# Sliding-window attention and a gated FFN: the values with their operands exchanged, and batch 0 taken unit by unit

## The chip, the core and the metric

The kernel runs on one core of one Trainium2 chip. A core has TensorE (matrix products, results into PSUM), VectorE, ScalarE and GpSimd (elementwise work), and queues that start transfers between the main memory (HBM) and the on-chip memory (SBUF, 128 partitions). The engines run side by side and wait for each other by semaphores. The metric is the device time of one execution in microseconds (us). In the profile the engines are called PE, DVE, ACT and POOL in this order; PEld is the loading of TensorE's stationary operand.

## What is computed

```python
# q, k, v: (8 batches, 8 heads, 576 positions, 64 wide), fp32
scores = (1/8) * q @ k.T                       # per batch and head
mask   = (rel >= 0) & (rel < 64)               # rel = query position - key position
attn   = softmax(where(mask, scores, -1e9))
a      = attn @ v
x      = a.transpose(0, 2, 1, 3).reshape(4608, 512)       # tokens x (heads * 64)
out    = (maximum(x @ w_gate, 0) * (x @ w_val)) @ w_out   # 512 -> 1536 -> 512, fp32
```

Each query sees only the 64 keys up to its own position. A block of 64 queries therefore needs 128 keys: the 64 before the block and the block's own.

## The kernel before

All 4608 tokens are cut into 24 units of 192 positions (three to a batch, all 8 heads) and 12 FFN tiles of two units (384 tokens). The operands are fp16, sums are fp32. The program gives each engine its order of instructions through a small scheduler: `W.at(t, fn)` puts the attention's steps at planned times between the matmuls of the FFN, which move the plan's clock forward; `ready(n)` makes the FFN wait until n units are finished.

For a unit, the scores come out with the keys on the partitions (so p has 128 keys x 64 queries for each window and head), in four row tiles of TensorE, since k and q lie in 32 partitions a head with the 64 channels in pairs:

```python
nc.tensor.matmul(d["st"][hh][g][:, c:c + 64],                        # L249
                 kT[rows, hh, ks + 64*w:ks + 64*w + 128, dh],        # rows: 32 partitions of head g
                 qT[rows, hh, ks + 64*w:ks + 64*w + 64, dh], ...)    # every second fp16 element
```

ScalarE takes the exponential into `p` (`u_exp`), VectorE multiplies by the band mask (`u_mask`). The values are then made with v stationary and p moving. v stands beside 64 columns of ones, so that one product gives the values of a head in 64 output partitions and the sum of p, repeated, in the other 64:

```python
def u_pv_wide(u):                       # 24 matmuls, units 2 to 23
    ...
    nc.tensor.matmul(d["pv"][c % 2][:, c // 2, e, 64*w:64*w + 64],   # L311
                     v16[:, w, 128*h - 64*e:128*h - 64*e + 128],     # 128 x 128 stationary: v and ones
                     d["p"][h % G][:, h // G, 64*w:64*w + 64], ...)  # 64 columns moving

def u_copy(u, n):    # ScalarE: values from PSUM to SBUF, twice two of 64 x 384             (L329)
def u_sum(u, half):  # VectorE: transposes the sums 32 x 32 out of PSUM, 64 x 384 each      (L341)
def u_back(u):       # VectorE: reciprocal of 24 numbers a partition, transposed back       (L348, L350)
def u_norm(u):       # VectorE: xt = values * reciprocal, 128 x 768, to fp16                (L356)
```

The result `xt` has the channels on the partitions, as the FFN needs them (`xt` is `[128, 4, 384]`: 4 groups of 128 channels). The units 0 and 1 do the same with other tiles of PSUM and separate matmuls with ones. v is loaded by windows of 64 keys into the upper 64 partitions, and `v_low` copies it to the lower 64 for the next window.

The FFN of a tile:

```python
def hidden(t, c0, c1, f0=0, f1=NF, each=1):    # NF = 12 blocks of 128 hidden columns
    ...
    nc.tensor.matmul(h[...], wt[:, c, 128*(f + b):128*(f + b) + 128],     # L419, wt: wg or wv
                     xt[:, c, c0:c1], start=(c == 0), stop=(c == NC - 1))
    # ScalarE: r_sb = relu(h of wg)    (L404);   VectorE: g_sb = r_sb * h of wv    (L407)

def output(t, subs):                           # 3 x 12 matmuls of 512 columns, g_sb stationary (L433)
    # ScalarE copies the result, the SP queue stores it
```

The start: k of batch 0 comes in fp32 whole, q of batch 0 whole with conversion to fp16 in the transfer; both are transposed by VectorE for all 576 positions; units 0 and 1 follow, then the FFN of the first half of tile 0.

```python
for hh in range(2): k_first(hh)
for hh in range(2): qk_load(0, "q", hh)
...
W.advance(13.7)
ready(1)
hidden(0, 0, U, 0, 4, 4)
ready(2)
hidden(0, U, TT, 0, 4, 4)
hidden(0, 0, TT, 4, NF, 4)
output_by_rows(0)
ready(3)
hidden(1, 0, U)
output(1, (0,))
ready(4)
hidden(1, U, TT)
output(1, (1, 2))
for t in range(2, NU // 2): ...
```

Of the kernel before, what the change touches and what calls it, by code (L numbers as in the profile page):

```python
# [9 lines left out]
FP32 = mybir.dt.float32  # L10
FP16 = mybir.dt.float16
ACT = mybir.ActivationFunctionType
MUL = mybir.AluOpType.mult

# [28 lines left out]
def kernel(  # L43
# [28 lines left out]
    a_16 = ctx.enter_context(tc.tile_pool(name="a_16", bufs=2))  # L72
    a_p = ctx.enter_context(tc.tile_pool(name="a_p", bufs=6))
# [13 lines left out]
    v16s = [persist.tile([128, UB, H, 128], FP16, name=f"v16_{i}") for i in range(UB)]  # L87
    ones0 = consts.tile([128, 64], FP16)
    ones = consts.tile([128, 64], FP16)
    mask = consts.tile([128, 64], FP16)  # L90
    bias = consts.tile([128, 64], FP16)
    ident = consts.tile([128, 128], FP16)

# [21 lines left out]
    def v_ones(i, eng):  # L115
        eng.memset(v16s[i][64 if i == 0 else 0:, 0, :, 64:128], 1.0)
        for w in range(1, UB):
            eng.memset(v16s[i][:, w, :, 64:128], 1.0)  # L118

    def k_zeros():  # L120
        nc.vector.memset(kTs[1][:, :, 0:64], 0.0)

    def constants():
        nc.vector.memset(kTs[0][:, :, 0:64], 0.0)
        nc.vector.memset(v16s[0][0:64, 0], 0.0)
        nc.vector.memset(ones, 1.0)
        nc.vector.memset(ones0, 1.0)
        nc.vector.memset(ones0[0:64], 0.0)
# [6 lines left out]
    def xt_tile(t):  # L135
        if t not in xts:
            xts[t] = x_sb.tile([128, NC, TT], FP16, name="xt")
        return xts[t]
# [4 lines left out]
    def w_load(wt, src, f0, f1, landed):  # L143

        sr = src.rearrange("(c p) n -> p c n", p=128)
        if wt is wo:
            dst, part = wo[:, f0:f1], sr[:, f0:f1]
        else:
            ns = slice(128 * f0, 128 * f1)
            dst, part = wt[:, :, ns], sr[:, :, ns]  # L150
        nc.gpsimd.dma_start(dst, part)
        w_done.update(((wt.name, f), landed) for f in range(f0, f1))
# [17 lines left out]
    def k_first(hh):  # L170

        k32 = nat["k32", hh] = x_sb.tile([128, S // 32 * D], FP32, name="k32", bufs=2)
        nc.sync.dma_start(k32, k[0, G * hh:G * hh + G].rearrange("h (i j) d -> (h i) (j d)", i=32))

    def k_round(hh, part, parts):
        n = S // 32 * D // parts
        if part == 0:
            nat[0, "k", hh] = a_in.tile([128, S // 32 * D], FP16, name=f"k{hh}", bufs=2)
        nc.scalar.copy(nat[0, "k", hh][:, n * part:n * part + n], nat["k32", hh][:, n * part:n * part + n])  # L179
# [8 lines left out]
    def v_load(u):  # L188
        b, uu = divmod(u, UB)
        for w in range(UB):  # L190
            k0 = U * uu + 64 * w
            nc.gpsimd.dma_start(v16s[uu][64:128, w, :, 0:64], v[b, :, k0:k0 + 64].rearrange("h p d -> p h d"))  # L192

    def v_low(u):

        uu = u % UB
        if uu > 0:
            nc.vector.tensor_copy(v16s[uu][0:64, 0, :, 0:64], v16s[uu - 1][64:128, UB - 1, :, 0:64])
        nc.vector.tensor_copy(v16s[uu][0:64, 1:UB, :, 0:64], v16s[uu][64:128, 0:UB - 1, :, 0:64])

    def u_bias(u, gs=range(G)):

        d = units.setdefault(u, {})
        if "st" not in d:
            st_tiles(u)
        d["biased"] = True
        for to in d["st"][0] + d["st"][1] if u == 0 else [d["st"][0][g] for g in gs]:
            n = 1 if u == 0 else 2
            nc.tensor.matmul(to[:, 0:n * U].rearrange("p (n c) -> p n c", c=64), ident,
                             bias[:, None, :].to_broadcast([128, n * UB, 64]),  # L210
                             start=True, stop=False, skip_group_check=True)
# [5 lines left out]

    def st_tiles(u):
        d = units.setdefault(u, {})
        one = lambda name: f_ps.tile([128, 512], FP32, name=name, tag="h")  # L220
        two = lambda name: a_ps.tile([128, 2, 512], FP32, name=name, tag="a")
        if u == 0:
            d["st"] = [[one("st") for _ in range(G)]]
            halves = [two("st") for _ in range(2)]
            d["st"].append([halves[g // 2][:, g % 2] for g in range(G)])
        elif u == 1:
            half = two("st")
            d["st"] = [[half[:, 0], half[:, 1], one("st"), one("st")]] * 2
        else:
            halves = [two("st") for _ in range(2)]  # L230
            d["st"] = [[halves[g // 2][:, g % 2] for g in range(G)]] * 2
        if u == 0:
            d["spare"] = d["st"][1][3][:, 256:512]
            d["st"] = [[x[:, 0:512 if hh == 1 and g == 3 else 256] for g, x in enumerate(row)] for hh, row in enumerate(d["st"])]

    def u_st(u, hhs=(0, 1)):
        d = units.setdefault(u, {})
        kT, qT = kTs[(u // UB) % 2], qTs[(u // UB) % 2]
        biased = "biased" in d
        if not biased:  # L240
            st_tiles(u)
        ks = U * (u % UB)
        for hh in hhs:
            for w in range(UB):
                c = U * (hh if u else 0) + 64 * w
                for dh in range(2):
                    for g in range(G):
                        rows = slice(32 * g, 32 * g + 32)
                        nc.tensor.matmul(  # L249
                            d["st"][hh][g][:, c:c + 64],  # L250
                            kT[rows, hh, ks + 64 * w:ks + 64 * w + 128, dh],
                            qT[rows, hh, ks + 64 * w:ks + 64 * w + 64, dh],
                            start=(dh == 0 and not biased), stop=(dh == 1),
                            skip_group_check=biased)
        d.setdefault("p", [None] * G)
        return 0.49

    def u_exp(u, g, hh=None):
        d = units[u]
        if not hh:  # L260
            d["p"][g] = a_p.tile([128, 2, U], FP16, name="p")
        if hh is None:
            nc.scalar.activation(d["p"][g].rearrange("p h c -> p (h c)"), d["st"][0][g][:, 0:2 * U], ACT.Exp, scale=scale)  # L263
        else:
            nc.scalar.activation(d["p"][g][:, hh], d["st"][hh][g][:, 0:U], ACT.Exp, scale=scale)

    def u_mask(u, g):
        p = units[u]["p"][g]
        p = p.rearrange("p h (w c) -> p (h w) c", w=UB)
        nc.vector.tensor_tensor(p, p, mask[:, None, :].to_broadcast([128, 2 * UB, 64]), MUL)  # L270

    def u_pv(u, cs=(0, 2, 1, 3)):
        if u > 1:
            return u_pv_wide(u)
        d = units[u]
        v16 = v16s[u % UB]
        if u == 0 and cs[0] == 0:
            d["pv"] = [f_ps.tile([128, 2, U], FP32, name="pv", tag="h") for c in cs]
        elif u == 0:
            both = a_ps.tile([128, 2, 512], FP32, name="pv", tag="a")  # L280
            d["pv"] += [both[:, n, 0:2 * U].rearrange("p (s c) -> p s c", s=2) for n in range(2)]
        else:
            halves = [a_ps.tile([128, 2, 512], FP32, name="pv", tag="a") for _ in range(2)]
            d["pv"] = [halves[c % 2][:, c // 2, 0:2 * U].rearrange("p (s c) -> p s c", s=2) for c in range(NC)]
        for c in cs:
            for w in range(UB):
                for e in range(2):
                    h = 2 * c + e
                    nc.tensor.matmul(
                        d["pv"][c][64 * e:64 * e + 64, 0, 64 * w:64 * w + 64],  # L290
                        v16[:, w, h, 0:64], d["p"][h % G][:, h // G, 64 * w:64 * w + 64],
                        start=(w == 0), stop=True, skip_group_check=True)
            for w0, w1, one in ((0, 1, ones0), (1, UB, ones)) if u % UB == 0 else ((0, UB, ones),):
                for e in range(2):
                    h = 2 * c + e
                    nc.tensor.matmul(
                        d["pv"][c][64 * e:64 * e + 64, 1, 64 * w0:64 * w1],
                        one, d["p"][h % G][:, h // G, 64 * w0:64 * w1],
                        start=False, stop=True, skip_group_check=True)
        return 1.2  # L300

    def u_pv_wide(u):

        d = units[u]
        v16 = v16s[u % UB].rearrange("p w h d -> p w (h d)")
        d["pv"] = [a_ps.tile([128, 2, 2, 256], FP32, name="pv", tag="a") for _ in range(2)]
        for c in (0, 2, 1, 3):
            for e in range(2):
# [317 lines left out]
```

The softmax here doesn't subtract the row's maximum and nothing guards it: scores larger than these inputs give would overflow.

## Time and profile before

| | |
|---|---|
| time, median of 3 runs | 339.22 us (339.13 to 339.65) |
| profiled run: time, span from first to last instruction | 339.75 us, 337.9 us |
| granted TensorE clock, mean | 0.994 |
| first matmul of the FFN | 17.00 us |
| last matmul | ends at 334.28 us |
| FFN hidden matmuls, 128 x 384, from the groups | 1024 of them, 326 ns each in the record |
| gate on VectorE, 128 x 384 out of PSUM | 550 ns, 144 of them |
| exponential on ScalarE, 128 x 384 out of PSUM | 492 ns, 92 of them |

How to read it: matmuls are pipelined, so the duration in the record (326 ns) is longer than the distance from one to the next; for the pace take the length of an uninterrupted piece in the chain of work that ended last, divided by its count. A group's line names line, engine, operation, output and input with partitions x elements, then the count, the busy time, the mean of one, and the idle time of the engine just before it with what ended that.

### The profile page before, as it was taken

Reading aid. Unit: us, or ns where it says so; the run is one execution under the profiler, and the core shown is the slowest. Engines: PE = TensorE matmul, PEld = TensorE weight load, DVE = VectorE, ACT = ScalarE, POOL = GpSimd, SP = SyncE. Lnnn points to the kernel's source line nnn. Section 1 sums busy time; section 2 is a strip of 40 time slices with the busy share of each in tenths; the row PEclk is TensorE's granted clock in tenths of the full one; section 3 lists DMA queues with packets and bytes.
Section 4 is the critical chain, followed back from the end, with each engine's and each line's share of the span. In section 5 each row is a group of like instructions: output and inputs, shape, how many; then the busy total and the mean of one; then the engine's idle time right before and its main releaser. Section 6 shows DMA issues by size and latency. Waiting matters only on the chain.

```text
span 337.9 us, 8605 instructions
## 1 busy us (share of the span) xinstructions
PE 325.5 (96%) x3522; PEld 197.3 (58%) x3522; DVE 260.3 (77%) x493; ACT 176.7 (52%) x383; POOL 74.0 (22%) x121
## 2 busy tenths in 40 slices
PE   8699998999999999999999999999999999999995
PEld 4485485856546656655655655654655664664653
DVE  5878878998998874897989974888889874884430
ACT  4546165745636646645555564564564664653321
POOL 8724341250213221320210410150120200000000
PEclk9989999999999999999999999999999999999999
DMA  8999998496343933491242853296214402001002
GB/s 214 178 206 193 204 203 135 31 139 98 24 77 49 158 51 71 29 185 70 17 53 73 111 75 98 18 143 123 17 10 111 32 3 93 2 2 71 24 0 94
DMA packets 52886, 29.44 MB, mean 87 GB/s; under 512 B 39280, under 2 KB 44272, under 8 KB 52848
## 3 DMA queue, kind: packets, MB, share of 16 engines
q0 software_dynamic: 47088, 18.29, 47.4%
q1 hardware_dynamic: 5616, 10.55, 8.7%
q8 instruction: 27, 0.44, 0.6%
q14 instruction: 11, 0.09, 0.1%
q10 hardware_dynamic: 144, 0.07, 0.1%
HBM read 37.75 MB, written 9.44 MB: 140 GB/s over the span
## 4 chain that ended last, share of the span: by engine, by line
PE 81%; DVE 13%; issue 3%; DMA 2%; ACT 0%; DVEq 0%; ACTq 0%; POOLq 0%
PE h L419 52%; PE op L433 21%; PE pv L311 5%; PE st L249 3%; DVE sT L341 2%; DVE qT L186 2%; DMA q<-in_q_dram 2%; DVE g_sb L407 2%; DVE kT L186 1%; DVE xt L356 1%; DVE rs L350 1%; DVE p L270 1%; PE op L465 1%; DVE v L118 1%; DVE rT L348 0%
## 5 line engine op out<-in xcount | busy, mean ns | idle before, releaser
L419 PE MATMUL h<-xt,wg 128*128 128x384 f16 (+1 forms) x640 | 117.5, 313 | 1.7 <-DVE xt L356 1.7
L419 PE MATMUL h<-xt,wv 128*128 128x384 f16 (+1 forms) x640 | 116.7, 311 | 1.0 <-DVE g_sb L407 1.0
L407 DVE TENSOR_TENSOR g_sb<-r_sb,h 128x384 f16<-128x384 f32 x144 | 78.3, 550 | 48.8 <-PE h L419 47.1
L404 ACT ACTIVATE r_sb<-h 128x384 f32<-128x384 f32 x144 | 70.2, 492 | 67.0 <-PE h L419 55.3
L433 PE MATMUL op<-wo,g_sb 128*128 128x512 f16 x420 | 93.0, 379 | 0.0
L192 POOL DMA_DIRECT2D v<-in_v_dram x72 | 49.5, 696 | 181.0 <-PE pv L311 95.3
L419 PEld LDWEIGHTS <-wg 128*128 128x128 f16 x640 | 61.5, 99 | 36.5 <-DVE xt L356 1.6
L419 PEld LDWEIGHTS <-wv 128*128 128x128 f16 x640 | 59.0, 98 | 31.7 <-issue 1.3
L433 PEld LDWEIGHTS <-g_sb 128*128 128x128 f16 x420 | 40.3, 98 | 46.6
L341 DVE STREAM_TRANSPOSE sT<-pv 64x384 f32<-64x384 f32 x88 | 51.1, 580 | 9.7 <-PE pv L311 7.7
L329 ACT COPY xv<-pv 64x384 f32<-64x384 f32 x88 | 41.6, 473 | 21.5 <-DVE sT L341 8.1
L440 ACT COPY o_sb<-op 128x512 f32<-128x512 f32 x35 | 20.5, 586 | 54.6 <-PE op L433 54.6
L263 ACT ACTIVATE p<-st 128x384 f16<-128x384 f32 x92 | 39.7, 492 | 4.2 <-PE st L249 4.1
L270 DVE TENSOR_TENSOR p<-p,mask 128x384 f16<-128x384 f16 x88 | 27.5, 352 | 0.3 <-ACT p L263 0.2
L350 DVE STREAM_TRANSPOSE rs<-rT 128x768 f32<-128x768 f32 x24 | 23.5, 978 | 0.8
L356 DVE TENSOR_TENSOR xt<-xv,rs 128x768 f16<-128x768 f32 x24 | 22.8, 948 | 0.8
L311 PEld LDWEIGHTS <-v 128*128 128x128 f16 x528 | 18.6, 98 | 4.2 <-issue 0.8
L186 DVE STREAM_TRANSPOSE kT<-k 128x576 f32<-128x576 f32 (+1 forms) x18 | 19.7, 1121 | 1.4 <-ACT k L179 1.3
L311 PE MATMUL pv<-p,v 128*128 128x64 f16 x528 | 19.7, 193 | 1.1 <-DVE p L270 0.6
L186 DVE STREAM_TRANSPOSE qT<-q 128x576 f32<-128x576 f32 x16 | 18.9, 1239 | 1.1 <-DMA q<-in_q_dram 1.1
L249 PEld LDWEIGHTS <-kT 32*128 32x128 f16 x1152 | 11.0, 92 | 10.0 <-issue 9.9
L249 PE MATMUL st<-qT,kT 32*128 32x64 f16 x1152 | 13.9, 189 | 2.3 <-DVE qT L186 2.0
(47 smaller groups left out, 91.8 us busy)
## 6 DMA issues: line engine op xcount, KB each, us to landing
out_dram<-o_sb SPq DMA_DIRECT2D x35, 256.0 KB, 2.0
q<-in_q_dram POOLq DMA_DIRECT2D x16, 288.0 KB, 8.1
v<-in_v_dram POOLq DMA_DIRECT2D x72, 64.0 KB, 3.2
k<-in_k_dram POOLq DMA_DIRECT2D x14, 288.0 KB, 6.1
wg<-in_moe_w_gate_dram POOLq DMA_DIRECT2D x3, 512.0 KB, 10.1
wv<-in_moe_w_val_dram POOLq DMA_DIRECT2D x3, 512.0 KB, 11.9
wo<-in_moe_w_out_dram POOLq DMA_DIRECT2D x3, 512.0 KB, 13.7
k<-in_k_dram SPq DMA_DIRECT2D x2, 576.0 KB, 4.0
```

Source lines behind the costliest of these rows:

```text
L186: nc.vector.transpose(dst.rearrange("p (i j) -> p j i", i=32)[:, j0:j1], src[:, j0:j1])
L192: nc.gpsimd.dma_start(v16s[uu][64:128, w, :, 0:64], v[b, :, k0:k0 + 64].rearrange("h p d -> p h d"))
L249: nc.tensor.matmul(d["st"][hh][g][:, c:c + 64], kT[rows, hh, ks + 64 * w:ks + 64 * w + 128, dh], qT[rows, hh, ks + 64 * w:ks + 64 * w + 64 ...
L263: nc.scalar.activation(d["p"][g].rearrange("p h c -> p (h c)"), d["st"][0][g][:, 0:2 * U], ACT.Exp, scale=scale)
L270: nc.vector.tensor_tensor(p, p, mask[:, None, :].to_broadcast([128, 2 * UB, 64]), MUL)
L311: nc.tensor.matmul(d["pv"][c % 2][:, c // 2, e, 64 * w:64 * w + 64], v16[:, w, 128 * h - 64 * e:128 * h - 64 * e + 128], d["p"][h % G][:, ...
L329: nc.scalar.copy(d["xs"][rows, n::2], d["pv"][n][rows, :, e, 0:U])
L341: nc.vector.transpose(to[64 * e:64 * e + 64, half::2], d["pv"][half][64 - 64 * e:128 - 64 * e, :, e, 0:U])
L404: nc.scalar.activation(part(r_sb), part(h1), ACT.Relu)
L407: nc.vector.tensor_tensor(g_sb[:, f:f + w, c0:c1], part(r_sb), part(h2), MUL)
L419: nc.tensor.matmul(h[:, b * n:b * n + n], wt[:, c, (f + b) * 128:(f + b) * 128 + 128], xt[:, c, c0:c1], start=(c == 0), stop=(c == NC - 1))
L433: nc.tensor.matmul(op, g_sb[:, f, bass.ds(sub * 128, 128)], wo[:, f], start=(f == 0), stop=(f == NF - 1))
```

## The change

It exchanges the operands of the value product. p is the stationary operand, 32 queries at a time, and v with one column of ones (65 columns) is moving; four heads stand side by side in the four column tiles of TensorE, so the output has 4 heads x 32 queries on the partitions and the channels, with the sum as the 65th column, along the row. The sum now lies in the partition of its query: the reciprocal and the normalisation need no transposes of sums. The normalised x (fp16) is transposed last, by VectorE, 32 x 32 words of two fp16 channels each. So `xt` becomes `[128, 2, 384, 2]`: a partition holds pairs of neighbouring channels, the FFN reads every second element, and the rows of w_gate and w_val are loaded in the matching order.

v is kept for a whole batch (9 windows of 128 keys, two batches of buffers), loaded by 128 keys for every other window; `v_spread` copies the rest, mostly on GpSimd.

Batch 0 is taken by units: k and q of unit 0 come in fp32 by themselves with all heads, are turned by TensorE (a product with a permuted identity) and copied to `kA` and `qA`; its scores use 64 partitions a head, two row tiles. The units 1 and 2 load and transpose their own parts of k and q. The FFN starts when the units 0 and 1 are both done. Later, the two units of a tile make their values together (`pair`).

```diff
-    a_p = ctx.enter_context(tc.tile_pool(name="a_p", bufs=6))
+    a_p = ctx.enter_context(tc.tile_pool(name="a_p", bufs=12))
-    v16s = [persist.tile([128, UB, H, 128], FP16, name=f"v16_{i}") for i in range(UB)]
+    VW = D + 2
+    v16s = [persist.tile([128, NG, H, VW], FP16, name=f"v16_{i}") for i in range(2)]
-            xts[t] = x_sb.tile([128, NC, TT], FP16, name="xt")
+            xts[t] = x_sb.tile([128, 2, TT, 2], FP16, name="xt")
...  # w_load of wg, wv: two transfers each
+            for a in range(2):
+                nc.gpsimd.dma_start(wt[:, 2 * a:2 * a + 2, ns], src.rearrange("(a p e) n -> a p e n", a=2, e=2)[a, :, :, ns])
...  # u_pv: 48 matmuls a unit
+        for hh in hhs:
+            for w in range(UB):
+                for s in range(2):
+                    for j in range(G):
+                        nc.tensor.matmul(
+                            to[32 * j:32 * j + 32, c:c + D + 1], d["p"][i][:, n, 32 * s:32 * s + 32],
+                            v16s[b % 2][:, vw, G * hh + j, 0:D + 1],
+                            start=True, stop=True, skip_group_check=True)
...  # u_recip, u_norm (twice a unit), u_turn: in place of u_copy, u_sum, u_back, u_norm
+            nc.vector.reciprocal(d["r"], d["both"][...][:, :, :, D:D + 1])
+        nc.vector.tensor_tensor(d["x"][:, hh], pv_of(d, u, hh)[:, :, 0:D],
+                                d["r"][:, hh].to_broadcast([128, SB, D]), MUL)
+        nc.vector.transpose(dst, d["x"][:, h0:h1].rearrange("p a s c -> p a (s c)").bitcast(FP32))
...  # the FFN's moving operand
-                                             xt[:, c, c0:c1], start=(c == 0), stop=(c == NC - 1))
+                                             xt[:, c // 2, c0:c1, c % 2], start=(c == 0), stop=(c == NC - 1))
...  # the start
+        for name in "kq":
+            all_load32(name, 0, nc.sync)
+            all_tile(name, 0)
...
+        for hh in range(2):
+            unit_load(1, "k", hh, 64)
+            unit_load(1, "q", hh)
+        v_load(0, ((1, 0, 128), (3, 0, 64)))
+        v_load(1, ((3, 64, 128), (5, 0, 128)))
+        w_load(*G3[0], 15.2)
+        w_load(*V3[0], 17.8)
+        for hh in range(2):
+            unit_load(2, "k", hh)
+            unit_load(2, "q", hh)
+        w_load(*G3[1], 22.5)
+        v_load(2)
+        w_load(*V3[1], 26.8)
+        w_load(*G3[2], 29.4)
+        w_load(*V3[2], 32.0)
...  # rounding, unit_flip (24 matmuls), unit_keep (copies out of PSUM) for k and q; first_st; unit 1
...  # the plan of the later units
+            W.at(P, lambda: u_pv(2 * t) + u_pv(2 * t + 1))
...
-        W.advance(13.7)
-        ready(1)
-        hidden(0, 0, U, 0, 4, 4)
+        W.advance(15.2)
         ready(2)
-        hidden(0, U, TT, 0, 4, 4)
-        hidden(0, 0, TT, 4, NF, 4)
-        output_by_rows(0)
+        hidden(0, 0, TT, 0, 8, 4)
         ready(3)
-        hidden(1, 0, U)
-        output(1, (0,))
+        hidden(1, 0, U, 0, 4, 4)
+        hidden(1, 0, U, 4, 8, 4)
+        hidden(0, 0, TT, 8, NF, 4)
+        hidden(1, 0, U, 8, NF, 4)
+        output(0)
         ready(4)
         hidden(1, U, TT)
-        output(1, (1, 2))
+        output(1)
```

## The prediction, made before the changed kernel ran

> **What bounds the kernel now.** I read the page's totals first, then the chain that ended last, then the same chain in order of time, then a table of busy times by stage.
>
> ```profile
> PE 325.5 (96%) x3522; PEld 197.3 (58%) x3522; DVE 260.3 (77%) x493; ACT 176.7 (52%) x383; POOL 74.0 (22%) x121
> ...
> PE 81%; DVE 13%; issue 3%; DMA 2%; ACT 0%; DVEq 0%; ACTq 0%; POOLq 0%
> ```
>
> TensorE is busy nearly always and is 81% of the chain; VectorE, with 13%, is the only other engine that holds the end back. So work taken from TensorE shortens the time one for one, and work taken from VectorE only where VectorE stands in the chain. One steady tile of 384 tokens, in the chain in order of time (start, length, what, count):
>
> ```profile
> 101.86 0.65 PE h L419 x4
> 102.51 0.48 PE st L249 x39
> 102.99 4.01 PE h L419 x24
> 107.00 0.70 PE pv L311 x24
> 107.70 7.80 PE h L419 x48
> 115.50 0.48 PE st L249 x39
> 115.98 3.36 PE h L419 x20
> 119.34 0.70 PE pv L311 x24
> 120.04 7.77 PE op L433 x36
> ```
>
> The reader is to see that a tile is a row of TensorE pieces with nothing between. 96 hidden matmuls of 384 columns take 7.80/48 = 0.1625 us each, 15.60 in all; 36 output matmuls take 7.77; a unit's scores 0.48 and its values 0.70. The FFN is 23.37 a tile, 12 x 23.37 = 280.4 us, and the change does not touch that arithmetic. The stages, by the places where the chain changes tile (columns: stretch, length, busy time of each engine, granted clock):
>
> ```profile
> 0.00:17.00 17.00, 12.86 (x214) 7.69 (x215) 11.95 (x28) 8.65 (x22) 13.45 (x27) 0.99 1.31 196
> 17.00:36.46 19.46, 18.96 (x201) 13.91 (x201) 15.30 (x34) 10.40 (x24) 6.47 (x10) 0.92 1.33 201
> ...
> 44.23:74.93 30.70, 28.23 (x445) 22.68 (x444) 26.59 (x53) 17.99 (x39) 11.28 (x19) 1.00 0.89 125
> 74.93:101.86 26.93, 26.42 (x279) 15.14 (x276) 24.35 (x43) 14.34 (x31) 3.41 (x5) 1.00 0.48 70
> 101.86:127.81 25.95, 25.95 (x278) 15.04 (x277) 20.50 (x41) 14.46 (x31) 6.97 (x11) 1.00 0.60 93
> ```
>
> The account of the 337.9 us span: 17.0 before the first FFN matmul (units 0 and 1 are done with TensorE by then), 280.4 of FFN, 22 units x 1.18 = 26.0, 3.6 after the last matmul, and so 10.9 of losses. By stage, length less FFN and units: 17.00 to 36.46 loses 19.46 - 16.78 = 2.7 (8% of it is the clock, 0.92: 1.6); 44.23 to 74.93 loses 30.70 - 26.91 = 3.8 (VectorE busy 26.6 of 30.7: it is the limit there); 74.93 to 101.86 loses 1.2; from there to 310.87, eight tiles, 3.2, of which 0.2 a tile is the change between kinds of matmul (25.95 against 25.73), and the rest the two tiles in which the next q and k are transposed.
>
> **What the Trainium skill says.** "TensorEngine Tiling (Array Packing)", "When to Use Tiling", names just this exchange: with 64 moving columns or fewer, swap stationary and streaming operand and tile by columns. Its "Restrictions" add that column tiling switches the fast weight load off. The trace has one hint: the values of unit 0 use two column tiles of 64, and ten such matmuls (eight of 64 columns, two of 128) come each 0.19 us, 19 ns apiece with a load of 64 columns each; so loads of 64 columns follow at 19 ns or less, and 32 columns should fit in some 10 ns. The same page's "Key Properties" says that a change of tiling mode drains the array; the 0.2 us a tile above fits that, though it is not proof. "SBUF — State Buffer", "Door 1: The DMA port swizzle", says that a strided read runs at full rate while two or more elements are taken from each 16-byte line. The new x is read at every second fp16 element, four per line, so at full rate. In the trace q is already read so by the scores: 48 matmuls of 64 columns in four row tiles take 0.48 us, 40 ns for four abreast, where half rate would need 64 x 2 / 2.4 = 53 ns. Half rate is ruled out, a milder slowdown isn't.
>
> **The change, part by part.**
>
> Values on TensorE. 24 matmuls of 64 columns (29 ns each, 0.70 us) become 48 of 65 columns in four column tiles. Abreast they are 12 groups; 65/2.4 = 27 ns each plus what the 48 issues ask. The scores issue 48 matmuls with 48 loads in 0.48, 10 ns apiece, and I take that: 0.48. Saved 0.22 a unit, 22 units: **4.8 us**, all on the path.
>
> VectorE and ScalarE. What goes:
>
> ```profile
> L341 DVE STREAM_TRANSPOSE sT<-pv 64x384 f32<-64x384 f32 x88 | 51.1, 580 | 9.7 <-PE pv L311 7.7
> L329 ACT COPY xv<-pv 64x384 f32<-64x384 f32 x88 | 41.6, 473 | 21.5 <-DVE sT L341 8.1
> ...
> L350 DVE STREAM_TRANSPOSE rs<-rT 128x768 f32<-128x768 f32 x24 | 23.5, 978 | 0.8
> L356 DVE TENSOR_TENSOR xt<-xv,rs 128x768 f16<-128x768 f32 x24 | 22.8, 948 | 0.8
> ```
>
> Per unit VectorE loses 4 x 0.58 + 0.98 + 0.95 = 4.25 us, and about 0.7 of v copies, which mostly go to GpSimd. It gains two normalisations of 384 elements out of PSUM (the gate of 384 elements takes 0.55: 1.1) and one transpose of 384 fp32 words (from 1.24 for 576 and 0.71 for 288: 0.89); the reciprocal stays near 0.3. Net about 2.9 us a unit, 5.8 a tile: VectorE falls from 20.5 to 24.4 of each 26 us to some 17. ScalarE loses 4 x 0.47 = 1.9 a unit, which was never the limit. Where VectorE was the limit this is worth: 44 to 75, loss 3.8 to 1.0; 75 to 102, 1.2 to 0.4; the eight later tiles, 3.2 to 2.0 (1.6 of changes of mode, 0.4 of batch ends). **4.8 us**.
>
> The start. Before, the first FFN matmul waits for k and q of the whole batch 0 (1.18 MB each in fp32), then transposes, scores, values, sums, and begins at 17.00 with unit 0 alone. After, only unit 0's k and q (2 x 0.39 MB, plain fp32) come first; they are turned on TensorE. My chain: k there at 4.0, q at 4.7; rounding (ScalarE took 0.67 for 576, so some 0.5 for 384) and 24 turning matmuls each, then copies out of PSUM at about 0.5: both kept by 7.5; scores 8.0; four exps at the 0.41 pace seen, 9.7. Meanwhile VectorE makes unit 1's four transposes, two of 256 and two of 192 words (0.65 and 0.53, 2.4): 9.9; its scores 10.4, exps 12.1, then two v copies on ScalarE 12.9; values 13.4. On VectorE the reciprocals and normalisations of unit 0 and its transpose end about 13.9, those of unit 1 (0.3 + 1.1 + 0.9) about 16.2. The FFN now needs both units, and starts at **16.3**, a gain of 0.7 only.
>
> Weights. By when the queue of transfers frees space, the six first weight pieces land in the kernel before at about 15.3, 18.3, 20.8, 23.4, 26.0 and 28.8: 2.55 us for each half megabyte. After, q and k of unit 2 (0.39 MB written) stand between the second and third, and v between third and fourth. The matmuls ask for the third 5.2 us after the start (21.5), the fourth 2.6 later. I estimate landings of 13, 15.5, 20.5 to 22 and 24 to 26: a wait of about 1.0, partly filled by unit 2. With a cold clock as before (1.6) the loss of the first stage stays 2.7, so the DMA wait eats what VectorE gives there.
>
> Sum: 16.3 + 280.4 + 22 x (0.48 + 0.48) + losses (2.7 + 1.0 + 0.4 + 2.0) + 3.6 = 16.3 + 280.4 + 21.1 + 6.1 + 3.6 = 327.5 us of span. The profiled run took 339.75 for a span of 337.9, so 1.85 on top, and the median lay 0.5 below that run: 328.9. I add 0.6 because more went into it at its best than at its worst: **329.5 us**, 2.9% less.
>
> **Rivals.**
> 1. *Weight loads become the bound of the values.* 48 loads of 128 x 32 without the fast path. If each costs 20 ns and nothing overlaps, a unit's values take 0.96 instead of 0.48: 22 x 0.48 = 10.6 us more, 340. For: the skill's restriction. Against: the 19 ns per instruction with twice the columns.
> 2. *Strided x slows the FFN.* 1152 matmuls of 384 columns stand on it; each per cent is 1.9 us, so 6% would turn the change into nothing. Against: the scores' pace and the 16-byte line. I give it 1 in 15.
> 3. *The start is bound by transfers.* v comes in packets of 128 bytes and shares the queue; if v of unit 0 or the third and fourth weight pieces come 2.5 us late, the time is 332 to 334. For: the transfer engines are busy from 2 to 40 us at about 200 GB/s. Against: less of k and q stands ahead of them (two units of batch 0, not three).
> 4. *VectorE was hidden anyway.* If the losses of 44 to 102 come from order on PSUM buffers and not from VectorE's load, only the values' 4.8 and the start are won: 332.
>
> **Range and chances.** Rivals 3 and 4 together put the time at about 335; values at 0.42 a unit, an earlier start by 1 and no DMA wait put it at 325. So 325 to 335. Below 332.4 it is faster by over 2%: 0.77; within 2%: 0.18; slower, which needs rival 1 or 2 at full size: 0.05.
>
> **What would show it.** In the changed kernel's chain, pieces of values of 0.96 us for a pair of units (1.08 or more speaks for rival 1); hidden matmuls still at 0.1625 us (rival 2 otherwise); the first of them at 16 to 17, and waits on weight transfers of about 1 us before 30 (rival 3: 3 us or more); no VectorE piece in the chain from 75 on, and VectorE near 205 us in all; tiles from the fourth on 25.5 us apart. The prediction is wrong if the first FFN matmul comes after 18.5, or if these tiles are 26 apart.

## The result, and the profile after

The changed kernel takes 341.60 us (median of 4, 340.80 to 341.98) against 339.21 before (339.13 to 339.65): a ratio of 1.0065, with a 95% interval from 1.0045 to 1.0085. It is slower, by little; the prediction was 329.5, in a range from 325 to 335.

The page of the changed kernel, totals and shares of the chain that ended last:

```profile
PE 326.5 (96%) x4041; PEld 184.7 (54%) x4041; DVE 188.3 (55%) x385; ACT 134.1 (39%) x285; POOL 97.6 (29%) x144
...
PE 90%; DVE 3%; DMA 2%; POOL 2%; ACT 1%; issue 0%; ACTq 0%; POOLq 0%
```

VectorE did lose 72 us of work and nearly all its share of the chain (13% to 3%), and ScalarE lost 43. TensorE, which the values should have relieved, is busy for 1 us more. One steady tile of the changed kernel, from the chain in order of time (start, length, what, count):

```profile
102.50 9.52 PE h L454 x56
112.02 0.48 PE st L304 x47
112.50 2.82 PE h L454 x16
115.32 0.48 PE st L304 x47
115.80 2.82 PE h L454 x16
118.63 0.94 PE pv L361 x89
119.56 1.46 PE h L454 x8
121.03 7.77 PE op L468 x36
```

The values of two units are now one piece of 0.94 us where there were two of 0.70: that is the gain, 0.46 a tile. But 56 hidden matmuls take 9.52 us, 0.170 each, not 0.1625. With 96 in a tile that is 0.72 more. The output matmuls (7.77) and the scores (0.48) stand as before, so it is no matter of the clock. The tile comes to 26.30 us (102.50 to 128.80) against 25.95.

The start of the same chain, with the steps of "issue" left out:

```profile
7.39 7.76 DMA v<-in_v_dram
...
15.18 0.62 ACT v L255
...
15.82 0.63 ACT v L257
...
16.48 0.77 PE pv L361 x40
...
17.54 1.03 DVE x L385 x2
...
18.60 0.59 DVE xt L394
...
19.23 6.90 PE h L454 x32
```

The last transfer of v lands at 15.15, two copies on ScalarE follow, then the values, the normalisation and the transpose of unit 1, and the first FFN matmul comes at 19.23, later than the 17.00 of before.

The account of the span, as the prediction set it up:

| term | predicted | measured |
|---|---|---|
| before the first FFN matmul | 16.3 | 19.23 |
| FFN, 12 tiles | 280.4 | 289.1 = 12 x (96 x 0.170 + 7.77) |
| 22 units, scores and values | 21.1 | 20.9 = 22 x (0.48 + 0.47) |
| losses | 6.1 | 7.8 (the rest) |
| after the last matmul | 3.6 | 3.3 |
| span | 327.5 | 340.3 |

Of the 12.8 us by which the span was missed, 8.7 are the pace of the FFN and 2.9 the start.

### The profile page after: what moved, and what is told of

The parts are those of the page before. It is cut to its first block, busy times and chain, and to the rows that moved or that the text cites. A ratio compares the mean times of both kernels' runs of the same rounds, so it can differ in the third digit from the quotient of the medians.

```text
span 340.3 us, 9389 instructions
## 1 busy us (share of the span) xinstructions
PE 326.5 (96%) x4041; PEld 184.7 (54%) x4041; DVE 188.3 (55%) x385; ACT 134.1 (39%) x285; POOL 97.6 (29%) x144
## 4 chain that ended last, share of the span: by engine, by line
PE 90%; DVE 3%; DMA 2%; POOL 2%; ACT 1%; issue 0%; ACTq 0%; POOLq 0%
PE h L454 58%; PE op L468 25%; PE pv L361 3%; PE st L304 3%; DMA v<-in_v_dram 2%; DVE p L339 2%; PE op L500 1%; ACT p L335 1%; POOL v L246 1%; DVE x L385 1%; POOL ku L179 0%; POOL qu L179 0%; DVE xt L394 0%; ACT v L257 0%; ACT v L255 0%
## 5 line engine op out<-in xcount | busy, mean ns | idle before, releaser
L454 PE MATMUL h<-xt,wg 128*128 128x384 f16 (+1 forms) x624 | 120.8, 321 | 2.7 <-DVE xt L394 2.7
L454 PEld LDWEIGHTS <-wg 128*128 128x128 f16 x624 | 58.6, 97 | 42.7 <-issue 4.5
L246 POOL DMA_DIRECT2D v<-in_v_dram x41 | 34.4, 852 | 81.8 <-PE pv L361 74.6
L339 DVE TENSOR_TENSOR p<-p,mask 128x384 f16<-128x384 f16 x88 | 32.2, 393 | 16.5 <-ACT p L335 16.2
L255 POOL COPY v<-v 64x512 f16<-64x512 f16 (+1 forms) x20 | 14.8, 739 | 43.4 <-DMA v<-in_v_dram 43.1
L385 DVE TENSOR_TENSOR x<-pv,r 128x384 f16<-128x384 f32 x48 | 25.0, 552 | 0.8
L361 PE MATMUL pv<-v,p 128*32 128x65 f16 x1152 | 13.6, 199 | 4.0 <-ACT v L257 1.9
L240 DVE STREAM_TRANSPOSE kT<-k 128x576 f32<-128x576 f32 x14 | 17.3, 1234 | 0.0
L361 PEld LDWEIGHTS <-p 128*32 128x32 f16 x1152 | 11.6, 97 | 9.0 <-issue 3.9
L257 POOL COPY v<-v 64x512 f16<-64x512 f16 (+1 forms) x20 | 15.4, 771 | 0.9
L394 DVE STREAM_TRANSPOSE xt<-x 128x384 f32<-128x384 f32 x24 | 13.9, 577 | 0.7
```

The costliest lines, as they stand in the source:

```text
L240: nc.vector.transpose(dst.rearrange("p (i j) -> p j i", i=32)[:, j0:j1], src[:, j0:j1])
L246: nc.gpsimd.dma_start(v16s[b % 2][lo:hi, g, :, 0:64], v[b, :, 64 * g - 64 + lo:64 * g - 64 + hi].rearrange("h p d -> p h d"))
L361: nc.tensor.matmul(to[32 * j:32 * j + 32, c:c + D + 1], d["p"][i][:, n, 32 * s:32 * s + 32], v16s[b % 2][:, vw, G * hh + j, 0:D + 1], star ...
L385: nc.vector.tensor_tensor(d["x"][:, hh], pv_of(d, u, hh)[:, :, 0:D], d["r"][:, hh].to_broadcast([128, SB, D]), MUL)
L454: nc.tensor.matmul(h[:, b * n:b * n + n], wt[:, c, (f + b) * 128:(f + b) * 128 + 128], xt[:, c // 2, c0:c1, c % 2], start=(c == 0), stop=( ...
```

## Experiments

The theory was that the hidden matmuls are slow since they read x at every second element (A). The rival was something else that the change brought to the FFN, such as the new order of the weights' rows or other engines' use of the memory (B). I tested it from both sides: the step taken out of the changed kernel, and put alone into the kernel before.

**x_read_contiguous**

```diff
-  xt[:, c // 2, c0:c1, c % 2]
+  xt.rearrange("p a t e -> p a (t e)")[:, c // 2, 2*c0 + (c % 2)*(c1 - c0):2*c0 + (c % 2 + 1)*(c1 - c0)]
```

> The changed kernel, but the FFN reads 384 (or 192) neighbouring fp16 elements of the same stretch of xt, not every second one; the tokens are then mixed, so what is left out is the right pairing of data, and no instruction is added or taken away. Theory A (the read at every second element slows each hidden matmul from 0.1625 to 0.170 us): the pace in the last tile goes back to 0.1625 us, 15.60 us for 96, and the time falls by 1152 x 7.5 ns = 8.6 us to about 333.0 us. Theory B (something else slows the FFN: the new order of the weights' rows, or other engines on the memory): pace 0.170 and 341.6 us as before.

Measured: 333.68 us (332.86 to 334.93), 0.9824 of before (0.9793 to 0.9855), 7.9 less than the changed kernel. The last tile, in its chain:

```profile
306.54 15.60 PE h L454 x96
```

96 in 15.60: the old pace. The weights' rows keep their new order in this kernel, and every other engine does the same work, so B falls.

**before_step_2**

```diff
-  xts[t] = x_sb.tile([128, NC, TT], FP16, name="xt")
+  xts[t] = x_sb.tile([128, NC, TT, 2], FP16, name="xt")
-  nc.vector.tensor_tensor(xt_tile(u // 2)[:, :, c0:c0 + U], d["xs"], rs, MUL)
+  nc.vector.tensor_tensor(xt_tile(u // 2)[:, :, c0:c0 + U, 0], d["xs"], rs, MUL)
-  xt[:, c, c0:c1]
+  xt[:, c, c0:c1, 0]
```

> The kernel before, with xt laid out with one unused fp16 element after each (step of 2 elements); all else the same. Theory A: hidden matmuls at 0.170 us, the time rises by some 8.6 us to about 347.8 us (a little less where the start and VectorE hide it). Theory B: 0.1625 us and 339.2 us, apart from what the normalisation's write at a step costs VectorE.

Measured: 347.17 us (346.52 to 347.76), 1.0229 of before (1.0202 to 1.0255), 7.9 more. The last tile:

```profile
318.22 16.32 PE h L419 x96
```

The step alone, in a kernel without any other part of the change, gives 0.170 us a matmul. (VectorE writes x at a step too, in 1015 ns in place of 948; the 96 matmuls above follow each other without a break, so that is not in them.) Theory A is shown from both sides.

**before_step_4** and **before_step_3**: the same edit with 4 and 3 in place of 2, one run each, to see what law it follows.

> The same with a step of 4 elements (8 bytes; two elements in each 16-byte line). If the rule of two elements per line were the whole law, the pace is as with a step of 2 or 1 (0.1625 to 0.170). If the slowdown grows with the bytes spanned, it is well above 0.170: 7.5 ns per doubling gives 0.178 to 0.185, and a read bound by lines gives up to 0.32.

> The kernel before with xt at a step of 3 elements (6 bytes). Measured: step 1 0.1625 us a hidden matmul, step 2 0.170, step 4 0.340. Theory A (the slowdown goes with the count of 16-byte lines a matmul reads: a line every two columns at step 4): step 3 reads a line every 2.67 columns, so 0.75 x 0.340 = 0.255 us, time some 440 us. Theory B (a cliff: up to some width at nearly full rate, beyond it half rate): 0.170 to 0.18 (about 350 us) or 0.340 (540 us).

Measured: 541.44 us with a step of 4 and 443.14 with a step of 3. Their last tiles, step 4:

```profile
495.52 32.64 PE h L419 x96
```

and step 3:

```profile
405.31 24.53 PE h L419 x96
```

| step | bytes covered (384 x 2 x step) | a matmul of 384 | per 16 bytes |
|---|---|---|---|
| 1 element | 768 | 0.1625 us | |
| 2 | 1536 | 0.1700 us | 1.77 ns |
| 3 | 2304 | 0.2555 us | 1.77 ns |
| 4 | 3072 | 0.3400 us | 1.77 ns |

From step 2 to step 4, the time is in proportion to the stretch of memory that the operand covers, 1.77 ns for every 16 bytes of a partition; the cliff that one theory of step 3 expected isn't there. If the proportion holds for a dense operand too (an estimate; no run shows it, and larger steps were not run), that would take 0.085 us to read, and is limited by its 384 columns; at step 2 the reading takes 0.170, just over the 0.1625 of the columns. By this account the loss is only 4.6% and easy to overlook.

**turn_16_bit**: can the exchange be kept with a dense x? The transpose is done on 16-bit elements, with even and odd channels as two planes. The rows of the weights can stay as the change has them.

```diff
-  dst = xt_tile(u // 2).bitcast(FP32).rearrange("p a t e -> p a (t e)")[:, h0:h1, c0:c0 + U]
-  nc.vector.transpose(dst, d["x"][:, h0:h1].rearrange("p a s c -> p a (s c)").bitcast(FP32))
+  for hh in range(h0, h1):
+      dst = xt_tile(u // 2)[:, 2*hh:2*hh + 2, c0:c0 + U].rearrange("p b (s q) -> p b s q", q=32)
+      nc.vector.transpose(dst, d["x"][:, hh].rearrange("p s (i b) -> p b s i", b=2))
#  xt is [128, NC, TT], and the FFN reads xt[:, c, c0:c1]
```

> The changed kernel with the transpose of x done on 16-bit elements, even and odd channels of a head as two planes, so that xt is contiguous again and the computation is whole; the transpose reads 384 fp16 elements at a step of two, twice a unit, in place of 384 words once. Theory A: FFN pace 0.1625, about 333.0 us, plus at most 0.6 us at the start for the longer transposes (1.2 us a unit against 0.58). Theory B: 341.6 us or more. If 16-bit transposes were much slower than 0.6 us each, VectorE would be seen in the chain.

Measured: 334.72 us (334.31 to 335.44), 0.9865 of before (0.9839 to 0.9890). This version computes the whole reference and is faster than both kernels. Run again as **turn_16_again**:

> turn_16_bit once more, beside warm_again on the same chip: 334.7 us.

Measured: 333.89 us (333.66 to 335.14), 0.9843 (0.9817 to 0.9868). The longer transposes, from the groups of the first run by shape (busy time and mean ns after the bar):

```profile
L395 DVE STREAM_TRANSPOSE xt<-x 128x384 f16<-128x384 f16 x48 | 24.7, 552 | 0.0
```

Two of 0.55 us a unit in place of one of 0.58 cost VectorE 11 us in all and the path little: x_read_contiguous, with the one transpose, took 333.68. In the chain of turn_16_again the outputs of two tiles begin at

```profile
92.69 7.77 PE op L469 x36
...
118.28 7.77 PE op L469 x36
```

25.59 us apart: 25.95 before, 26.30 in the changed kernel. So the exchange of operands, with the values of two units made together, does gain 0.36 us a tile, and the strided x spent twice that.

**The start.** Theory A here: the first FFN matmul is late because transfers land late and hinder each other. Theory B: the order of work on ScalarE and VectorE sets it. Both experiments stand on turn_16_bit, where the FFN began at 18.85.

**no_v_at_start**

```diff
-  v_load(0, ((1, 0, 128), (3, 0, 64)))
-  v_load(1, ((3, 64, 128), (5, 0, 128)))
+  nc.vector.memset(v16s[0][:, 1:6]..., 0.0)     # ahead of v_fixed
```

> turn_16_bit without the four transfers of v of the units 0 and 1 (their v is zero; the computation of these tokens is left out), copies and matmuls kept. There the first FFN matmul came at 18.85 us, with q and k of unit 1 landing up to 11.1. Theory A (the start is bound by transfers, v slows q and k of unit 1): these land by 9 to 10, the first FFN matmul comes at 17.8 or before. Theory B (the order of work on ScalarE and VectorE sets the start): 18.5 to 19.

Measured, in one run: 334.38 us, the FFN begins at 18.45. q and k of unit 1 still land up to 11.31, and fp32 q of unit 0 at 7.53. So v does not slow these, and taking its transfers away brings 0.4 us: behind v's landing stood the exponentials of unit 1 and, after them on ScalarE, the two copies of v, which end only 0.2 us earlier than in the kernel with v.

**no_qkv_at_start**: also without the transfers of q and k of unit 1 (`gpsimd.memset` of their tiles in their place).

> turn_16_bit without the transfers of v of the units 0 and 1 and of q and k of unit 1 (all zero; these tokens' computation is left out); only k and q of unit 0 and the weights are loaded ahead of the FFN. Measured with them: fp32 q of unit 0 there at 6.7 to 7.5 us, q and k of unit 1 at 11.1 to 11.3, first FFN matmul at 18.45 (without v) and 18.85 us. Theory A (the prediction's working of 16.3 was right in its steps on the engines and wrong in when the transfers land): q by 5.5, first FFN matmul at 16.5 or before. Theory B (the steps on the engines themselves take longer): 17.5 or later.

Measured, in one run: 331.96 us. VectorE's and TensorE's instructions in order of time (start, length, what; in brackets the wait before it and what ended it):

```profile
6.86 0.36 DVE L203 CAST qa<-q 128x384 f16<-128x384 f32 x1 [1.28 <-DMA q<-in_q_dram]
```

```profile
13.61 0.55 PE L361 MATMUL pv<-v,p 128*32 128x65 f16 x25 [1.03 <-ACT v L257]
15.15 0.41 PE L361 MATMUL pv<-v,p 128*32 128x65 f16 x15 [0.99 <-issue]
17.43 4.03 PE L455 MATMUL h<-xt,wg 128*128 128x384 f16 x16 [1.87 <-DVE xt L395]
```

The first FFN matmul comes at 17.43, between the two theories. q of unit 0 still lands at 6.86. That does not show how soon it would land alone: in this run the first weights are issued at 3.17 us (9.46 in the changed kernel), so they move beside q. The transfers of unit 1 and v cost 1.4 us (18.85 to 17.43). Another 1.0 us is a stop of TensorE in the middle of unit 1's values, for which the trace names no releaser. It stands on the path: without it the FFN would have begun at about 16.4 (an estimate, 17.43 less 0.99), near the 16.3 of the prediction.

**The clock.** In turn_16_bit the first 16 FFN matmuls take 5.07 us where 2.6 would do, and the table by stage shows a granted clock of 0.50 from 14 to 22 us (the third figure from the end of the line):

```profile
18.85:22.00 3.15, 3.15 (x10) 1.43 (x10) 1.35 (x4) 0.89 (x2) 2.30 (x4) 0.50 1.30 177
```

**warm_start**: matmuls on zeros in TensorE's waits before the FFN.

```diff
   u_bias(1)
+  heat(12, spare1, False)
   u_st(1)
+  heat(10, spare1, False)
...
   u_turn(0)
+  heat(14, spare1, False)
   u_pv(1)
+  heat(24, spare1, False)
```

> turn_16_bit with 60 added matmuls on zeros, of 128 columns, in TensorE's waits before the first FFN matmul, so that the clock is not lowered there (it was 0.50 from 14 to 22 us). Theory A (the first FFN block, 5.07 us for its first 16 matmuls in place of 2.6, is slow for the lowered clock alone): 2.5 us less, about 332.2 us. Theory B (it waits for weights or PSUM, the clock is only shown low): no gain, 334.7, or some tenths more for the added matmuls.

Measured: 333.74 us, but from 332.41 to 336.40. The granted clock is up:

```profile
18.00:22.00 4.00, 3.52 (x25) 2.04 (x23) 2.25 (x5) 1.75 (x4) 3.00 (x4) 1.00 1.32 180
```

As the spread is wide, I ran it again beside turn_16_again, as **warm_again**:

> warm_start once more: its first profiled run held a gap of 2.5 us at 115 us in which TensorE waited for nothing shown, so its 333.7 us was unclear. Without such a gap: 332.4 us, 2.3 less than turn_16_again (theory A, the clock); equal to it if the clock is not the cause.

Measured: 334.38 us (333.91 to 334.85) against 333.89: no gain. The lowered clock was the cause of the slow first block, though. TensorE's instructions, here of warm_again,

```profile
18.83 2.90 PE L455 MATMUL h<-xt,wg 128*128 128x384 f16 x16 [0.48 <-DVE xt L395]
```

show the first 16 in 2.9 us, and turn_16_again has

```profile
18.86 4.94 PE L455 MATMUL h<-xt,wg 128*128 128x384 f16 x16 [1.87 <-DVE xt L395]
```

The 2.0 us won shrink to 1.1 by the start of tile 1's second half (55.41 against 56.50), since the FFN now waits for weights twice, 0.9 us together, and then this, in warm_again's chain, takes back the rest:

```profile
114.85 0.78 PE pv L361 x65
115.63 1.50 issue
117.13 0.33 PE pv L361 x16
```

In warm_start there is a gap of 2.50 us after the same matmul. It costs more than itself: the granted clock falls to 0.50 behind it, and the next eight hidden matmuls take 2.54 us, where warm_again's take 1.31 after its 1.50. TensorE waits for nothing that the profile shows. But the places of these stops have a pattern. I counted TensorE's recorded instructions (loads, matmuls and waits) ahead of each stop that has no releaser. It is 3266 in both warm runs here, 450 in both at 16.1 us, 449 for the stop in no_qkv_at_start at 15.15 and for one in no_v_at_start, 2498 and 2497 for others near 90 us: whole multiples of 256 apart, within one. Stops at fixed places of the stream of instructions speak for instructions that arrive late, in blocks of 256. Why they come late at some of these places and in some runs (turn_16_again has no such stop) stays open.

**turn_16_warm_half**: warm, the FFN begun with unit 0 alone, and unit 3 planned earlier.

```diff
+  ready(1)
+  hidden(0, 0, U, 0, 4, 4)
   ready(2)
-  hidden(0, 0, TT, 0, 8, 4)
+  hidden(0, U, TT, 0, 4, 4)
+  hidden(0, 0, TT, 4, 8, 4)
#  the matmuls on zeros of warm_start stay, 6 in place of the last 24;
#  and 2.5 off the planned times of unit 3 and of batch 1's q and k transposes
```

> turn_16_bit, warm as in warm_start, the FFN begun with unit 0 alone (192 columns, as in the kernel before), and unit 3 planned 2.5 us earlier, so that the first FFN matmul need not wait for unit 1 and tile 1 not for unit 3 (a wait of 1.8 us there). Expected: warm 2.5, first matmul 1.3 to 1.6 earlier, unit 3 up to 1.8: about 329.0 us. If transfers of weights are the limit from 17 to 30 us, the first two come back as waits and it is 331 to 332.

Measured: 334.75 us (334.61 to 334.88), 0.9858 (0.9837 to 0.9880), no better than turn_16_bit. The FFN begins at 17.72 instead of 18.85, and the gain comes back as waits; TensorE's list of whom it waited for (us in total, times, longest) begins

```profile
PE h L455 <- DVE g_sb L443: 1.6, 1, 1.6
PE st L304 <- DVE qT L233: 1.5, 2, 1.3
PE h L455 <- DMA wv<-in_moe_w_val_dram: 1.3, 2, 1.0
```

The weights arrive no sooner (1.3): TensorE takes up the fourth piece of them at 29.48, and at 29.47 in warm_again, where the FFN began 1.1 later. So up to 30 us the transfers set the pace, as the expectation allowed for. But it put the time at 331 to 332 for that case, and the rest is the earlier unit 3: a transpose of k, now ahead of a gate on VectorE, waits 1.85 us there for k to land, and TensorE waits 1.6 for the gate; then unit 3's scores wait 1.0 for the transpose of q and its values 0.9 for the masks. Tile 1's second half begins at 58.10, 2.7 us later than in warm_again.

## Why the prediction was wrong, step by step

The step that failed is the first below: the prediction kept the FFN at 0.1625 us a hidden matmul while its operand went to every second element, and it took 0.170. Both signs that the prediction named against itself came: the first FFN matmul after 18.5 (19.23), and later tiles 26 apart (26.30).

- **The FFN's arithmetic is not touched by the change: wrong, and the whole sign hangs on it.** The prediction named the strided x as rival 2 and gave it 1 in 15. It rested on a line of the skill, that two elements from each 16-byte line are enough for full rate ("SBUF — State Buffer", "Door 1: The DMA port swizzle"). The same passage goes on that each access that crosses to a new line pays a penalty, which the prediction left out. The measurement decides: four in a line cost 4.6%, two in a line 109%. It rested further on the scores' pace with a strided q, and that evidence could not tell: 64 columns at a step of 2 cover 256 bytes, which read in 28 ns by the 1.77 ns above, well inside the 40 ns that four matmuls abreast take anyway (if the four read side by side, as one after another they would need 113). My own text said that a mild slowdown was not ruled out; 96 matmuls a tile made a mild one worth 8.7 us.
- **The start at 16.3: 19.23.** The steps on the engines were near (1.9 us for the last three on VectorE, where 2.3 was said). What was mis-sized were the landings, which I had guessed and not taken from a row: fp32 q of unit 0 at 6.7 (4.7 in my working), v at 15.15 (not on my path at all). After v came the two copies, put ahead of the values and now behind the landing. Rival 3 had the right cause for 1.4 us, as no_qkv_at_start shows; there the FFN began at 17.43, and 1.0 of that is the stop without a releaser.
- **Values at 0.48 a unit: right.** 0.94 us for the pair. The loads of 32 columns, without the fast path by the skill ("TensorEngine Tiling (Array Packing)", "Restrictions"), showed no cost: 96 matmuls with their loads in 0.94 us are 9.8 ns apiece. Rival 1 falls.
- **VectorE's relief: right in its work, overrated in its worth.** VectorE is busy for 188 us. The 205 of the prediction does not follow from its own working: 2.9 us a unit are 70 us for 24 units, which leaves 191. The last transpose takes 0.58 and not 0.89; it writes dense words, while the rows I scaled from write at a step, and row L341 of my own list, also 384 words, had 0.58. No VectorE piece stands in the chain of the steady tiles, and the eight later tiles lose 2.5 against 3.2, with 2.0 predicted. From 44 to 75 us the loss is 2.5 and not 1.0: 1.5 of it lies between 46.7 and 56.9, where unit 3 comes late: its values are spread over 1.16 us in place of 0.47, and then the FFN waits 0.65 for its transpose. From 44 to 102 together the loss fell from 5.0 to 3.1, where 1.4 was predicted. Rival 4 is neither shown nor excluded: the changed kernel has less work for VectorE and another order too, and no run separates them.
- **The wait for weights, 1.0: none** in the changed kernel, whose FFN began late. Where it ran faster there (warm_again) or also began earlier (turn_16_warm_half), it appeared: 0.9 and 1.3. The lowered clock cost 1.5 (32 matmuls in 6.90 against 5.44), near the 1.6 predicted.

Without the step in x, prediction and kernel would have differed by 4 us: x_read_contiguous measured 333.7, inside the range.

## What to carry to other kernels

Price a new layout by the instructions that read it: a step in an operand read by 1152 matmuls outweighed all that the cheaper producer saved. Let the one cheap instruction that makes the data also sort it (here a transpose of 16-bit elements from a strided source), so that the many that read it find it dense. And a pace that is hidden under another limit, like that of the strided q, is no evidence that the pace is full.

## What the runs showed of the hardware that I had not expected

A moving operand of 384 fp16 columns, read at a step of 2, 3 or 4 elements, takes 1.77 ns for each 16 bytes of a partition that it covers (0.170, 0.2555 and 0.340 us), at step 2 alike whether the elements between are used (the changed kernel) or not (before_step_2). A 32 x 32 transpose on VectorE of 384 16-bit elements read at a step of two takes 0.55 us, and one of 384 dense 32-bit words 0.58: in these two forms the cost goes by the element, not by the byte. And TensorE can stop for up to 2.5 us in a row of dense small matmuls with nothing in the trace to release it; in these runs such stops stand at multiples of 256 of its instructions from each other, within one.
